# 56 short products behind the first products of ones, at the start of an attention and expert kernel

## The chip, the cores and the metric

The kernel runs on one core of a Trainium2 chip. Its time is device time in microseconds (us), as the median of several runs. The core has a matrix engine (TensorE, PE in the profile; its weight loads are listed apart as PEld), a vector engine (VectorE, DVE), a scalar engine (ScalarE, ACT), GpSimd (POOL) and SyncE (SP), whose queue issues most of the DMAs.

## What is computed

The reference joins two blocks. The first is linear attention without a softmax over 8 batches, 8 heads, 576 rows and 64 columns a head, followed by a normalisation of each row of a head:

```python
kv = np.einsum('bhsd,bhse->bhde', k, v)
out = np.einsum('bhsd,bhde->bhse', q, kv)
rms = np.sqrt(np.mean(out * out, axis=-1, keepdims=True) + 1e-06)
return (out / rms * g_norm).astype(np.float32)
```

Its result, laid out as 4608 tokens of 512, is the input of the second. Each token gets one of 8 experts: all pairs of token and expert are taken in falling order of their logits, and a pair is accepted if the token is free and the expert holds fewer than 576 tokens. Then each expert works on its own tokens:

```python
logits = x @ w_gate
...
h = np.maximum(x[mask] @ w1[e], 0.0)
out[mask] = h @ w2[e]
```

## The kernel before

**Attention.** A batch's Q, K and V are loaded in two halves each, of 576 KB, by `load` (line 84). The order is K, V, Q of the first half and then of the second. The first two batches are issued at once, the batch `b + 2` at the end of the function `prepare(b)`. `paced` (line 76) lets a load wait for the one three before it. For each batch `prepare` does, on TensorE: the sums K'V of four pairs of heads (`sum_kv`, line 342, whose products are on line 346), the turning of Q (`turn_q`, line 327, products on line 331), the turning of the sums (line 385) and the product of the sums with the gate's weights (line 395). `tiles` (line 410) multiplies the turned Q by the sums (line 434), and ScalarE, VectorE and GpSimd normalise the result. The main loop (lines 512 to 529) takes a piece of `prepare(b + 1)` behind every piece of the work on batch `b`, so that the two alternate on TensorE.

The order of instructions on TensorE, VectorE, ScalarE and SyncE is that of the program text in this part (`tc.manual_schedule`, line 508). TensorE starts with batch 0 alone, since nothing else is loaded: `prepare(0)` runs to its end first. Between its steps stand products of a tile of ones by another (`ones`, line 266), 9, 3, 4 and 3 of them. Each multiplies `ones_b` (128 by 128, bf16) by `wide` (128 by 512, bf16) into the first half of `begun`, a tile of PSUM. Nothing reads that half. The second half of `begun` takes the bound on the gate's logits (`gate_bound`, line 280).

Each product on TensorE is two instructions in the program, a weight load (LDWEIGHTS) and the product itself (MATMUL).

**Experts.** After the attention part the kernel chooses the experts' tokens by a search for thresholds (lines 575 to 700 or so; its counting products, of 128 by 32 weights with 8 columns, are on line 584), gathers the tokens, and multiplies them expert by expert (lines 1005, 1110 and 1124), with the second product's results scattered to the output by GpSimd (line 922). A last block, `exactly`, is there for inputs on which the search didn't settle; a branch passes it here.

The change touches `prepare` and adds a function beside `ones`.

Of the kernel before, what the change touches and what calls it, by code (L numbers as in the profile page):

```python
# [28 lines left out]
def kernel(  # L29
# [11 lines left out]
    nc = tc.nc  # L41
# [4 lines left out]
    E, _, F = moe_w1.shape  # L46
# [37 lines left out]
    def load(name, b, h):  # L84

        if h == 0:
            loaded[name, b] = att.tile([P, NP, R, D], FT, name=f"{name}_sb", tag=name, bufs=2)
        rs = slice(h * NP // 2, (h + 1) * NP // 2)
        src = {"k": k, "v": v, "q": q}[name]
        paced(nc.sync.dma_start(  # L90
            loaded[name, b][:, rs].rearrange("p r j d -> p r (j d)"),
            src[b].rearrange("h s d -> (h s) d").rearrange("(r p j) d -> p r (j d)", r=NP, j=R)[:, rs]))
# [50 lines left out]
    ones_b = asg.tile([P, P], BF, name="ones_b")  # L143
    nc.vector.memset(ones_b, 1.0)
    wide = asg.tile([P, 512], BF, name="wide")
# [118 lines left out]
    begun = psa.tile([P, 2, 512], FT, name="begun_ps", tag="o", bufs=2)  # L264

    def ones(times):

        for _ in range(times):
            nc.tensor.matmul(begun[:, 0], lhsT=ones_b, rhs=wide, start=True, stop=True)

    g2_ps = begun[:, 1, 0:E]

    def gate_norms():

        nc.vector.tensor_scalar(gw.rearrange("p r l e -> p (r l e)"), in0=gw.rearrange("p r l e -> p (r l e)"),
                                scalar1=g_col, scalar2=None, op0=AL.mult)
        nc.vector.tensor_tensor(gsq, gw.rearrange("p r l e -> p (r l e)"), gw.rearrange("p r l e -> p (r l e)"), op=AL.mult)
        nc.vector.reduce_sum(out=g2, in_=gsq.rearrange("p (a e) -> p e a", e=E), axis=AXX)
# [39 lines left out]
    def prepare(b):  # L318

        k_sb, v_sb = loaded.pop(("k", b)), loaded.pop(("v", b))  # L320

        q_sb = loaded.pop(("q", b)).rearrange("p r j d -> p (r j d)")
        NT = NP * R // 2
        qt = att.tile([P, 2, NT, HP], FT, name="qt", tag="qt", bufs=3)
        turned_q[b] = qt

        def turn_q(n):
            m = min(4, NT - 4 * n)
            t_ps = psa.tile([P, 4, P], FT, name="qt_ps", tag="tr", bufs=2)
            for x in range(m):  # L330
                nc.tensor.transpose(t_ps[:, x, :], q_sb[:, (4 * n + x) * P:(4 * n + x + 1) * P], ident)  # L331

            to, got = qt[:, :, 4 * n:4 * n + m], t_ps[:, 0:m].rearrange("p x (l c) -> p l x c", l=2)
            if n in (1, 2):
                nc.vector.tensor_copy(to, got)
            else:
                nc.scalar.copy(to, got)


        kv_ps = psa.tile([P, 2, 512], FT, name="kv_ps", tag="kv")  # L340

        def sum_kv(r):
            for j in range(R):
                for l in range(2):
                    ls, cs = slice(l * D, (l + 1) * D), slice(j % 2 * D, (j % 2 + 1) * D)
                    nc.tensor.matmul(kv_ps[cs, l, r * D:(r + 1) * D], lhsT=k_sb[ls, r, j, :], rhs=v_sb[ls, r, j, :],  # L346
                                     start=(j < 2), stop=(j >= R - 2))

        if b == 0:
            ones(9)  # L350
            sum_kv(0)
            sum_kv(1)
            ones(3)
            turn_q(0)
            turn_q(1)
            gate_norms()
            ones(4)
        else:
            sum_kv(0)
            turn_q(0)  # L360
            yield
            sum_kv(1)
            turn_q(1)
            if b % 2 == 0:
                yield
        sum_kv(2)
        sum_kv(3)
        odd = att.tile([D, 2, NP * D], FT, name="odd", tag="odd")
        nc.scalar.copy(odd, kv_ps[D:P, :, 0:NP * D])
        kv = att.tile([D, NP, 2, D], FT, name="kv", tag="kv")  # L370
        nc.vector.tensor_tensor(kv.rearrange("p r l d -> p l r d"),  # L371
                                kv_ps[0:D, :, 0:NP * D].rearrange("p l (r d) -> p l r d", d=D),
                                odd.rearrange("p l (r d) -> p l r d", d=D), op=AL.add)

        kvx = att.tile([P, H, W], FT, name="kvx", tag="kvx", bufs=3)
        for n in range(2):
            nc.gpsimd.tensor_copy(kvx[n * D:(n + 1) * D, :, 0:D], kv.rearrange("p r l d -> p (r l) d"))  # L377
        if b > 0:
            yield
        else:  # L380
            ones(3)
        turn_q(2)
        t_ps = kv_ps[:, 0, NP * D:2 * NP * D].rearrange("p (r d) -> p r d", d=D)
        for r in range(NP):
            nc.tensor.transpose(t_ps[:, r, :], kv[:, r].rearrange("p l d -> p (l d)"), ident[0:D, 0:D])
        kvt = att.tile([P, NP, D], FT, name="kvt", tag="kvt")
        nc.scalar.copy(kvt, t_ps)
        if b > 0:
            yield
        else:  # L390
            turn_q(3)
        w_ps = kv_ps[:, 1, NP * D:NP * D + NP * 2 * E].rearrange("p (r x) -> p r x", r=NP)
        for r in range(NP):
            for n in range(2):
                nc.tensor.matmul(w_ps[n * D:(n + 1) * D, r], lhsT=kvt[:, r, :],
                                 rhs=gw[:, r].rearrange("p l e -> p (l e)"), start=True, stop=True)
        nc.vector.tensor_copy(kvx[:, :, D:W], w_ps.rearrange("p r (l e) -> p (r l) e", l=2))
        kv_of[b] = kvx
        if b > 0:
            turn_q(3)  # L400
        turn_q(4)
        if b + 2 < B:
            for h in range(2):
                for name in "kvq":
                    load(name, b + 2, h)
# [102 lines left out]
    with tc.manual_schedule(engines={PE, DVE, ACTE, SPE}):  # L508
        for _ in prepare(0):
            pass  # L510
        gate_bound()
        for b in range(B):
            parts = prepare(b + 1) if b + 1 < B else iter(())
            n = 0
            tile_work = work(b)
            for _ in tile_work:
                next(parts, None)
                n += 1
                if b == 0 and n == 1:
                    columns()  # L520
                for _ in range(((0, 1, 2, 2), (0, 1, 2, 0, 2))[b % 2][n - 1] if b + 1 < B else (0, 1, 1, 0, 0)[n - 1]):
                    chosen()
            while b + 1 == B and choices:
                chosen()
            for do in late:
                do()

            while b + 2 >= B and writes:
                writes.pop(0)()
# [845 lines left out]
```

## Time and profile before

| | us |
|---|---|
| median of 3 runs | 606.0 |
| lowest and highest run | 605.68 and 615.02 |
| the profiled execution's own time | 605.56 |
| its span, from the first to the last instruction | 603.7 |
| mean granted clock of TensorE | 0.971 |
| TensorE busy (products) | 569.0, 4524 instructions |
| TensorE busy (weight loads) | 448.9, 4524 instructions |
| VectorE, ScalarE, GpSimd busy | 388.0, 184.4, 413.2 |

The span is 1.86 us shorter than the profiled execution's time. The attention part takes the first 110 us or so, the choice of the tokens the next 25, the experts the rest.

The profile's views are read like this. The page gives each engine's busy time and count of instructions, and the span in 40 slices of 15.1 us, whose digits are tenths (9 is 90% or more); the row PEclk is the clock that TensorE was granted. In a timeline a row has the start in us, the length in us, the engine, the line of the program, the operation, the output and inputs, the shape, the count of instructions merged into the row, and in square brackets the idle time ahead of it with what ended that. The chain of waits is the work that ended last, followed back from the end; "issue" in it is time in which an engine waited for nothing that the profile shows. A row of windows has the window, its length, then for PE, PEld, DVE, ACT and POOL the busy time and in brackets the count of instructions, and last the granted clock, the share of the DMA engines and GB/s.

### The profile page before, as it was taken

The page shows a single profiled execution, that of the slowest core. Times are in us where ns is not written, and L with a number is a line of the kernel's source. Part 1 is how long each engine was busy: PE and PEld are TensorE (multiplying, and loading weights), DVE is VectorE, ACT ScalarE, POOL GpSimd, SP SyncE. Part 2 cuts the span into 40 slices and gives each one's busy share as a digit, 9 for nine tenths or more (in the row PEclk, how much of TensorE's full clock was granted, in tenths as well). Part 3 has the DMA queues.
Part 4 walks back from the last instruction along what each step waited for, and adds up shares of the span by engine and source line. Part 5 has one row for each costly group of instructions (what it writes and reads, how often), then busy time and mean ns, then how long its engine had stood idle before and what let it go on. Part 6 is the DMA issues. An engine that isn't in the chain of part 4 may idle for free.

```text
span 603.7 us, 12101 instructions
## 1 busy us (share of the span) xinstructions
PE 569.0 (94%) x4524; PEld 448.9 (74%) x4524; DVE 388.0 (64%) x1195; ACT 184.4 (31%) x417; POOL 413.2 (68%) x367
## 2 busy tenths in 40 slices
PE   6899899458999999999999999999999999999995
PEld 3788788435788678867877786788678867877883
DVE  3676558768878797878767875887583355134411
ACT  1566456813221322232122203221322222223200
POOL 0146435215998989479969796987898699869523
PEclk9999799659999999999999999999999999999999
DMA  8998988948027169159538617580949364310002
GB/s 282 326 317 293 308 295 298 341 140 278 4 80 277 71 143 327 53 144 284 167 78 280 175 62 179 184 231 1 272 136 258 65 218 130 108 53 27 1 0 84
DMA packets 60932, 105.24 MB, mean 174 GB/s; under 512 B 5312, under 2 KB 19904, under 8 KB 60864
## 3 DMA queue, kind: packets, MB, share of 16 engines
q1 hardware_dynamic: 54272, 85.47, 45.2%
q0 software_dynamic: 5888, 18.88, 9.8%
q8 instruction: 38, 0.62, 0.4%
q14 instruction: 30, 0.25, 0.1%
q10 hardware_dynamic: 704, 0.02, 0.1%
HBM read 78.40 MB, written 25.95 MB: 173 GB/s over the span
## 4 chain that ended last, share of the span: by engine, by line
PE 83%; DVE 6%; DMA 4%; issue 3%; POOL 2%; ACT 1%; POOLq 0%; DVEq 0%; ACTq 0%
PE h_ps L1005 34%; PE y_ps L1110 32%; PE o_ps L434 5%; PE y_ps L1124 4%; PE kv_ps L346 3%; DMA v_sb<-in_v_dram 3%; PE qt_ps L331 2%; DVE ms L450 1%; PE given_ps L588 1%; DMA g_col<-in_g_norm_dram 1%; PE given_ps L584 1%; DMA xg<-x_dram,ids 1%; PE t_ps L913 1%; POOL out_dram L922 1%; POOL sw L935 0%
## 5 line engine op out<-in xcount | busy, mean ns | idle before, releaser
L1005 PE MATMUL h_ps<-xt,w_sb 128*128 128x288 f32 x384 | 101.1, 412 | 0.9 <-ACT xt L916 0.8
L1017 ACT ACTIVATE hid<-hid 128x288 f32<-128x288 f32 x128 | 55.6, 443 | 149.9 <-DVE hid L1000 148.0
L1005 PEld LDWEIGHTS h_ps<-xt,w_sb 128*128 128x128 f32 x384 | 70.8, 190 | 24.9 <-issue 4.9
L1000 DVE TENSOR_TENSOR hid<-h_ps,u 128x288 f32<-128x288 f32 x128 | 56.8, 453 | 28.5 <-PE h_ps L1005 24.5
L1005 PE MATMUL h_ps<-sx,sw 128*128 128x288 f32 x256 | 68.1, 407 | 0.1
L811 POOL DMA_INDIRECT xg<-x_dram,ids x40 | 38.2, 955 | 33.9 <-DVE upper L641 21.7
L1110 PE MATMUL y_ps<-tw,hid 128*128 128x256 f32 x256 | 59.2, 381 | 0.0
L1110 PE MATMUL y_ps<-tw,sh 128*128 128x256 f32 x256 | 59.1, 381 | 0.0
L1005 PEld LDWEIGHTS h_ps<-sx,sw 128*128 128x128 f32 x256 | 48.3, 190 | 13.8 <-DVE u L1000 0.6
L1110 PE MATMUL y_ps<-w_sb,hid 128*128 128x256 f32 x256 | 58.3, 382 | 0.0
L475 POOL TENSOR_TENSOR xo<-o_sb,inv 128x512 f32<-128x512 f32 x31 | 32.5, 1077 | 30.3 <-ACT o_sb L442 12.7
L1110 PEld LDWEIGHTS y_ps<-w_sb,hid 128*128 128x128 f32 x256 | 48.0, 190 | 6.7
L1110 PEld LDWEIGHTS y_ps<-tw,sh 128*128 128x128 f32 x256 | 48.2, 190 | 6.4
L1110 PEld LDWEIGHTS y_ps<-tw,hid 128*128 128x128 f32 x256 | 48.1, 190 | 6.5
L1000 DVE TENSOR_TENSOR u<-h_ps,u 128x288 f32<-128x288 f32 x96 | 42.1, 450 | 11.4 <-PE h_ps L1005 9.0
L922 POOL DMA_INDIRECT out_dram<-y_sb,outs x32 | 31.7, 989 | 22.7 <-issue 21.6
L907 ACT ACTIVATE xt<-t_ps,g_two 128x256 f32<-128x256 f32 (+1 forms) x60 | 23.9, 450 | 65.0 <-DVE t_ps L904 56.7
L434 PE MATMUL o_ps<-kvx,qt 64*128 64x72 f32 (+1 forms) x640 | 41.1, 274 | 2.8 <-issue 1.4
L434 PEld LDWEIGHTS o_ps<-kvx,qt 64*128 64x128 f32 (+1 forms) x640 | 36.2, 182 | 7.0 <-issue 5.5
L935 POOL TENSOR_TENSOR tw<-w_sb 128x512 f32<-128x512 f32 x32 | 40.0, 1271 | 0.1
L1000 DVE TENSOR_TENSOR y_sb<-y_ps,u 128x512 f32<-128x512 f32 x24 | 16.5, 687 | 31.0 <-PE y_ps L1110 30.7
L377 POOL COPY kvx<-kv 64x512 f32<-64x512 f32 x16 | 9.8, 610 | 37.5 <-DVE kv L371 37.0
(216 smaller groups left out, 1065.8 us busy)
## 6 DMA issues: line engine op xcount, KB each, us to landing
w_sb<-in_moe_w_dram SPq DMA_DIRECT2D x8, 2048.0 KB
w_sb<-in_moe_w_dram SPq DMA_DIRECT2D x48, 256.0 KB
k_sb<-in_k_dram SPq DMA_DIRECT2D x16, 576.0 KB
v_sb<-in_v_dram SPq DMA_DIRECT2D x16, 576.0 KB
q_sb<-in_q_dram SPq DMA_DIRECT2D x16, 576.0 KB
x_dram<-xo SPq DMA_DIRECT2D x16, 512.0 KB
relaid<-xg SPq DMA_DIRECT2D x24, 256.0 KB
xr<-relaid SPq DMA_DIRECT2D x24, 256.0 KB
```

Source lines behind the costliest of these rows:

```text
L346: nc.tensor.matmul(kv_ps[cs, l, r * D:(r + 1) * D], lhsT=k_sb[ls, r, j, :], rhs=v_sb[ls, r, j, :], start=(j < 2), stop=(j >= R - 2))
L434: nc.tensor.matmul(o_ps[rows_at, rp, (2 * r2 + l) * W:(2 * r2 + l + 1) * W], lhsT=turned_q[bn][ks, l, block // 2:block // 2 + m].rearrange ...
L475: nc.gpsimd.tensor_tensor(xo[t // 2][:, t % 2], o_sb[:, t, :, 0:D], inv[:, t * H:(t + 1) * H].rearrange("p (h o) -> p h o", o=1).to_broadc ...
L811: tokens = nc.gpsimd.indirect_dma_start(out=xg[0:nr], out_offset=None, in_=x_dram, in_offset=bass.IndirectOffsetOnAxis(ap=ids[0:nr, n:n + ...
L907: nc.scalar.mul(xt[:, q::2, a:a + nr], t_ps[:, q::2, 0:nr], g_two[:, q:q + 1])
L922: put = nc.gpsimd.indirect_dma_start(out=out, out_offset=bass.IndirectOffsetOnAxis(ap=ids_of[t][0:nr, n:n + 1], axis=0), in_=y_sb[0:nr, :] ...
L935: in_order(nc.gpsimd.tensor_tensor(o, x, y, op=op))
L1000: nc.vector.tensor_tensor(o, p_ps, u, op=AL.add)
L1005: nc.tensor.matmul(o, lhsT=left[:, d, f * P:(f + 1) * P], rhs=right[:, d], start=d == 0, stop=d == KH - 1)
L1017: nc.scalar.activation(h, h, ACT.Relu)
L1110: nc.tensor.matmul(p_ps[:, n], lhsT=left[:, f, n * P:(n + 1) * P], rhs=right[:, f], start=(f == 0), stop=(f == FH - 1))
L1124: nc.tensor.matmul(y_ps[l * nr:(l + 1) * nr], lhsT=hid[:, l * FH + f, a:a + nr], rhs=w2[:, l * FH + f, :], start=(f == 0), stop=(f == FH - 1))
```

## The change

A function `short` is added beside `ones`. It issues products of the first 32 columns of `ones_b` by the first 8 columns of `wide`, into 32 rows and 8 columns of the half of `begun` that nothing reads. In `prepare(0)` it is called with 56, behind the first nine products of ones and ahead of the first sums. These are 56 weight loads and 56 products more in TensorE's stream. Nothing is removed or moved.

```diff
         for _ in range(times):
             nc.tensor.matmul(begun[:, 0], lhsT=ones_b, rhs=wide, start=True, stop=True)
 
+    def short(times):
+
+        for _ in range(times):
+            nc.tensor.matmul(begun[0:32, 0, 0:8], lhsT=ones_b[:, 0:32], rhs=wide[:, 0:8], start=True, stop=True)
+
     g2_ps = begun[:, 1, 0:E]
...
         if b == 0:
             ones(9)
+            short(56)
             sum_kv(0)
             sum_kv(1)
             ones(3)
```

## The prediction

> **What bounds the kernel now.** I read the page first, then the timeline of the first 25 us, the chain of waits, and windows of the stretches that these pointed to. From the page:
>
> ```profile
> span 603.7 us, 12101 instructions
> PE 569.0 (94%) x4524; PEld 448.9 (74%) x4524; DVE 388.0 (64%) x1195; ACT 184.4 (31%) x417; POOL 413.2 (68%) x367
> PEclk9999799659999999999999999999999999999999
> PE 83%; DVE 6%; DMA 4%; issue 3%; POOL 2%; ACT 1%; POOLq 0%; DVEq 0%; ACTq 0%
> q8 instruction: 38, 0.62, 0.4%
> ```
>
> TensorE carries 83% of the chain that ended last, so whatever is to change the time must shorten or lengthen TensorE's own stream, in a stretch where nothing else ends later. The clock is whole except in the slices around 60 to 90 us and 105 to 135 us. The change sits far ahead of both. The beginning, in the timeline of TensorE:
>
> ```profile
> 1.69 3.91 PE L269 MATMUL begun_ps<-wide,ones_b 128*128 128x512 bf16 x9 [1.69 <-DVE wide L146]
> 7.26 1.38 PE L346 MATMUL kv_ps<-v_sb,k_sb 64*64 64x64 f32 x72 [1.67 <-DMA v_sb<-in_v_dram]
> 12.64 1.38 PE L346 MATMUL kv_ps<-v_sb,k_sb 64*64 64x64 f32 x72 [1.15 <-DMA v_sb<-in_v_dram]
> 18.89 0.80 PE L346 MATMUL kv_ps<-v_sb,k_sb 64*64 64x64 f32 x36 [0.24 <-DMA v_sb<-in_v_dram]
> 24.14 1.38 PE L346 MATMUL kv_ps<-v_sb,k_sb 64*64 64x64 f32 x72 [0.85 <-DMA v_sb<-in_v_dram]
> ```
>
> The nine products of ones end at 5.60; the first real products start at 7.26, when V has landed. Three more waits for V follow, 1.15, 0.24 and 0.85 us, the last ending at 24.14. The chain of waits says the same and goes on:
>
> ```profile
> 12.61 6.14 DMA v_sb<-in_v_dram
> 18.77 5.24 DMA v_sb<-in_v_dram
> 24.14 1.38 PE kv_ps L346 x70
> ...
> 46.91 0.49 issue
> ...
> 63.30 1.61 issue
> ...
> 86.40 1.41 issue
> ...
> 99.23 1.31 PE kv_ps L346 x70
> ```
>
> Up to 24 us the chain is loads, and TensorE's delays vanish in it. From 24 us TensorE itself is the chain. In it stand three holes, 3.51 us in all, in which TensorE waits for nothing that the profile shows ("issue"), in the middle of groups of equal products. What they are is the main question here, since the change adds 112 instructions to TensorE's stream (56 weight loads, 56 products) and nothing else.
>
> **What the holes are.** Windows cut at the holes, whose counts in brackets are the products (first) and the weight loads (second) in each:
>
> ```profile
> 10.80:47.30 36.50, 32.67 (x762) 27.50 (x760) 24.63 (x72) 20.13 (x41) 11.29 (x14) 1.00 0.96 325
> 47.30:64.50 17.20, 15.64 (x381) 13.76 (x380) 12.15 (x31) 11.36 (x22) 8.45 (x10) 1.00 0.91 307
> 64.50:87.50 23.00, 21.49 (x379) 18.80 (x380) 13.30 (x37) 11.05 (x22) 10.41 (x11) 0.78 0.92 303
> ```
>
> Between the holes lie 761 and 759 instructions, and 1522, twice as many, back to 10.8. Holes that come at equal counts belong to the stream and not to the work. The page's queue q8 carries instructions in 38 packets, 0.62 MB together and so 16 KB each. A third of 761 is 254, and TensorE's 9048 (4524 weight loads and as many products) instructions are 35.6 times 254, near those 38. I take it that the stream arrives in pages of about 254 counted instructions, that entering one page asks for the next, and that a hole is a page that isn't there when the one before is used up. [...]
>
> How long a page takes is bounded by the stretches that end at the holes, which begin one page ahead of them, and by the quickest page without a hole:
>
> ```profile
> 41.73:47.30 5.57, 5.17 (x126) 4.42 (x127) 3.96 (x9) 3.40 (x7) 3.46 (x4) 1.00 0.93 312
> 58.99:64.50 5.51, 4.30 (x134) 3.75 (x134) 4.04 (x9) 4.24 (x8) 1.98 (x3) 1.00 0.94 333
> 80.05:87.50 7.45, 6.34 (x133) 5.45 (x130) 5.95 (x17) 4.92 (x10) 3.92 (x4) 1.00 0.90 301
> 87.80:92.27 4.47, 4.46 (x125) 4.01 (x128) 1.46 (x4) 2.88 (x6) 0.73 (x2) 1.00 0.80 243
> ```
>
> The holes end at 46.91 + 0.49 = 47.40, 64.91 and 87.81, so those pages took 5.7, 5.9 and 7.8 us from the entry of the one before; the last row had its page in at most 4.5. While the loads keep the DMA engines 90 to 96% busy, a page thus takes some 4.5 to 5.9 us, once 7.8, and TensorE uses one up in 4 to 6: it is close to starved all through the attention part.
>
> **The short products themselves.** Two rows are nearest: products of the very same shape (128 by 32 weights, 8 columns, bf16), from the chain, at half clock, and products with 64-column weights at full clock:
>
> ```profile
> 119.44 1.45 PE given_ps L584 x36
> 16.40 0.65 PE L395 MATMUL kv_ps<-gw,kvt 128*64 128x16 f32 x16
> ```
>
> That is 40 ns each at half clock; halved for the full clock 20 ns is the lower end, and the second row's 41 ns, an overestimate since it holds the last product's way out, agrees with the upper. 56 of them take 1.1 to 2.3 us and end between 6.7 and 7.9; I take 1.7, which ends about when V lands. At the worst the first sums start 0.6 us late. They have until 12.64: the wait of 1.15 there swallows it, and if that cover were gone, 0.24 and 0.85 us come behind it. No engine waits on the products' result and no DMA is issued by them; SP's and POOL's queues are not passed. Nothing below zero comes from here either: the sums can't start ahead of V. This term is 0.
>
> **The moved pages.** Each page edge behind the insertion now comes 112 instructions earlier in the work. The hole at 46.91 shows where: 113 counted instructions ahead of it is 45.13. From there on a page at a time (instructions that overlap an edge are counted on both sides of it):
>
> ```profile
> 45.13:47.30 2.17, 1.78 (x57) 1.40 (x56) 1.13 (x2) 1.13 (x2) 2.17 (x3) 1.00 0.91 289
> 45.13:49.31 4.18, 3.69 (x128) 3.25 (x128) 1.16 (x3) 1.71 (x3) 3.98 (x4) 1.00 0.91 305
> 56.62:60.53 3.91, 3.91 (x134) 3.53 (x134) 2.18 (x5) 2.46 (x5) 3.13 (x4) 1.00 0.89 275
> 69.40:76.16 6.76, 6.76 (x128) 5.85 (x129) 1.54 (x3) 1.71 (x3) 4.37 (x5) 0.50 0.93 295
> 83.82:89.55 5.73, 4.32 (x130) 3.90 (x131) 2.96 (x7) 2.31 (x5) 3.95 (x4) 1.00 0.86 293
> ```
>
> The three old holes go: -3.5 us. Against a page time of 4.5 to 5.9 us, the new page from 45.13 holds 4.18 - 0.49 = 3.7 us of work: a hole of 0.8 to 2.2. The one from 56.62 holds 3.9: 0.6 to 2.0. The one from 83.82 holds 5.73 - 1.41 = 4.3: 0.2 to 1.6. The rest of the new pages have 5 us or more, or lie past the loads. Together 1.6 to 5.8, middle 3.7. Net -1.9 to +2.3, middle +0.2.
>
> **The clock behind a hole.** The second hole is followed by a slow stretch:
>
> ```profile
> 66.00:67.00 1.00, 1.00 (x16) 0.84 (x14) 0.72 (x3) 0.95 (x3) 0.00 (x0) 0.91 0.91 336
> 76.00:78.00 2.00, 2.00 (x35) 1.81 (x29) 0.69 (x2) 0.67 (x2) 0.00 (x0) 0.74 0.97 345
> 60.28 1.05 PE o_ps L434 x16
> 70.03 1.92 PE o_ps L434 x16
> ```
>
> The clock, 0.50 between these windows, falls at 66.8 (0.91 of a window whose end runs at 0.5) and is back at 77.0: 10.2 us. The last two rows are the same group in the chain of waits, 1.92 us in the stretch against 1.05 ahead of it. So 0.55 of the slow time would have done, and the stretch costs 10.2 x 0.45 = 4.6 us. The holes of 0.49 and 1.41 us are followed by no fall. [...] My reading is that a hole of about 1.6 us can bring it on, depending on where it lies against some window. A new hole of up to 2.0 us after 60.53 is the heir of the old one at 63.30, at nearly the same place and of the same size. I expect the fall to stay, a few us earlier, at the same price: 0.
>
> **The sum.** 0 + 0.2 + 0 on the profiled execution's 605.56 us (603.7 of span and 1.86 around it), which is 0.4 under the median of 606.0 of runs from 605.68 to 615.02: about 606.0 on the median's scale.
>
> **Rivals.** (1) The fall of the clock goes: the new hole behind 60.53 is shorter, or is cut by a window's edge as the one at 86.40 may be. TensorE gains 4.6 us, if loads allow:
>
> ```profile
> 88.81 0.37 SPq L90 DMA_DIRECT2D v_sb<-in_v_dram  x1
> ```
>
> The last V is issued at 88.81; at the 5.2 us that such a load took at 18.77 it lands at 94.1, and it is used at 99.23, so up to 5.1 us can be won there before loads bind. But the page from 69.40 then holds 6.76 x 0.55 = 3.7 us and gets a hole of 0.8 to 2.2, say 1.5. -4.6 + 0.2 + 1.5 = -2.9: 603.1, between 600.5 and 605. For it: two of three holes brought no fall. (2) Slower: a second fall. It takes a hole of about 1.6 us at 49.31 or 89.55 as well, both within the upper end of their ranges; +0.2 + 4.6 = 610.8, more if the page of 7.8 us recurs. (3) The holes go not by count but by the DMA's load at that moment, and moving the edges does nothing: 606.0. Against it stand the equal counts. (4) The short products end so late that first sums pass 12.64: they would need over 1.15 + 1.67 = 2.8 us, 50 ns each, and even then 24.14 still takes the delay; I give it no chance of its own.
>
> **Chances.** Forecast 0.42 (604 to 608), clock's fall gone 0.27, second fall 0.18, nothing moves 0.08, and 0.05 for what lies past 2%. Two per cent, 12 us, is about what a measurement of this kernel can tell from no change. To go past it downward all holes and more than the clock's fall would have to go (0.02); upward takes three falls (0.04 with the second rival's tail). The range reaches over rivals 1 and 2 without their ends: 601 to 611.5.
>
> **What would show it.** Right: short products from about 5.6, the first sums at 7.3 to 7.9, a wait for V still ending at about 12.6 and 24.1; no hole at the groups that held the old ones, and new ones 112 instructions earlier in the work modulo a page, near 49 and 61; a stretch of half clock of some 10 us near 63 to 74. Wrong: a start of the fifth V group later than 24.2; holes still at the same groups; the end of the attention part (last use of V, 99.23) off by over 3 us; any difference behind 140 us.

## The result, and the profile after

The first measurement gave 613.22 us as the median of 4 runs (609.41 to 614.48) against 605.84 us of the kernel before (4 runs, 605.31 to 615.02); the ratio is 1.0116, interval 1.0073 to 1.0158. That lies above the range. In three later measurements of 10 to 12 runs each beside 29 to 31 of the kernel before, the ratio came out at 0.9992 (0.9944 to 1.0041), 1.0005 (0.9957 to 1.0053) and 0.9955 (0.9901 to 1.0009). These ratios leave out the runs over 1.5% above the fastest of a kernel, so that a kernel without a fast run keeps all of its runs (e10 and e14 below); here those runs are the upper end of one wide scatter, and medians over all runs stand beside the ratios: 607.8 us over 34 runs with the change, 612.0 over 88 without it, measured together. One more run of the kernel before took 1173.78 us at full clock; it is in none of the figures over several measurements. The change made no slower kernel; whether the lower median is a gain the ratios leave open. What the first eight runs showed is what this document has to explain.

The page of the changed kernel, in the profiled execution (612.97 us):

```profile
span 611.2 us, 12210 instructions
PEclk9997579958999999999999999999999999999999
PE 81%; DMA 8%; DVE 5%; POOL 2%; issue 2%; ACT 1%; POOLq 0%; ACTq 0%; DVEq 0%
```

Loads have gone from 4% to 8% of the chain, "issue" from 3% to 2%, and the clock's dip is wider. The beginning, in TensorE's timeline:

```profile
5.31 1.55 PE L274 MATMUL begun_ps<-wide,ones_b 128*32 128x8 bf16 x56
7.22 1.38 PE L351 MATMUL kv_ps<-v_sb,k_sb 64*64 64x64 f32 x72 [0.36 <-DMA v_sb<-in_v_dram]
13.58 1.38 PE L351 MATMUL kv_ps<-v_sb,k_sb 64*64 64x64 f32 x72 [2.10 <-DMA v_sb<-in_v_dram]
23.59 1.38 PE L351 MATMUL kv_ps<-v_sb,k_sb 64*64 64x64 f32 x72 [0.32 <-DMA v_sb<-in_v_dram]
```

The 56 products took 1.55 us, 28 ns each, and end at 6.86, ahead of V. The first sums start at 7.22 (7.26 before), and TensorE still waits for loads at 13.58 and 23.59. So the beginning costs nothing. The chain of waits further on:

```profile
41.76 5.44 DMA v_sb<-in_v_dram
47.19 0.14 issue
47.33 1.38 PE kv_ps L351 x70
48.71 1.04 PE o_ps L440 x15
49.75 0.83 issue
...
67.91 1.91 PE o_ps L440 x16
...
84.84 1.05 PE o_ps L440 x16
...
106.15 1.31 PE kv_ps L351 x70
```

Without the old holes TensorE keeps up with the loads, which stay the chain up to 47 us (24 before). Then one hole of 0.83 us comes at 49.75, and no other of that kind follows in the attention part. But the group on line 440 takes 1.91 us at 67.91 and 1.05 only at 84.84. The last use of V comes at 106.15, where it was at 99.23: 6.9 of the span's 7.5 us are lost by then. Windows show where; first two of the changed kernel, then two of the kernel before:

```profile
49.32:52.73 3.41, 2.58 (x34) 2.12 (x32) 2.85 (x8) 1.41 (x4) 1.83 (x3) 1.00 0.91 295
52.73:83.45 30.72, 30.72 (x413) 26.71 (x412) 13.61 (x36) 13.31 (x26) 10.65 (x11) 0.50 0.90 300
```

```profile
63.40:66.81 3.41, 1.91 (x27) 1.71 (x28) 2.23 (x7) 1.86 (x5) 0.00 (x0) 1.00 0.94 326
66.81:77.05 10.24, 10.24 (x184) 8.96 (x181) 3.53 (x8) 3.59 (x8) 5.26 (x5) 0.50 0.90 289
```

The clock, last number but two, fell at 52.73 and stayed at half for 30.72 us, against 10.24 before; TensorE was busy all the time in both. Of the 20.5 us more, 0.45 is lost (the share worked out in the prediction): +9.2. A hole of 0.83 us in the place of 3.51 us of holes gives -2.7. The sum, +6.5, is near the 6.9 lost by the last use of V. The lengths are 3 and 9 times 3.41 us. The later stretches at half clock, during the choice of tokens, are 7 and 6 times as long; first the kernel before, then the changed one:

```profile
111.18:135.08 23.90, 10.47 (x165) 6.81 (x165) 17.00 (x60) 11.73 (x45) 1.91 (x3) 0.50 0.60 224
```

```profile
120.99:141.47 20.48, 9.19 (x147) 6.06 (x145) 14.88 (x54) 9.22 (x39) 1.01 (x1) 0.50 0.42 159
```

The full clock between them, from 77.05 to 111.18 and from 83.45 to 120.99, lasts 10 and 11 times 3.41 us. So all changes of the clock in these two profiles lie a whole number of 3.41 us apart, and the windows of 3.41 us below are counted off from such a change. In the kernel before one begins at 87.29 (77.05 + 3 x 3.41), inside the hole of 1.41 us from 86.40 to 87.81.

### The profile page after: what moved, and what is told of

Its sections match the earlier page's. It is cut to its first block, busy times and chain, and to the rows that moved or that the text cites. A ratio compares the mean times of both kernels' runs of the same rounds, so it can differ in the third digit from the quotient of the medians.

```text
span 611.2 us, 12210 instructions
## 1 busy us (share of the span) xinstructions
PE 577.8 (95%) x4577; PEld 457.5 (75%) x4580; DVE 387.8 (63%) x1195; ACT 184.5 (30%) x417; POOL 412.5 (67%) x367
## 4 chain that ended last, share of the span: by engine, by line
PE 81%; DMA 8%; DVE 5%; POOL 2%; issue 2%; ACT 1%; POOLq 0%; ACTq 0%; DVEq 0%
PE h_ps L1011 34%; PE y_ps L1116 31%; DMA v_sb<-in_v_dram 7%; PE y_ps L1130 4%; PE o_ps L440 4%; PE kv_ps L351 3%; PE qt_ps L336 2%; DVE ms L456 1%; PE given_ps L594 1%; PE given_ps L590 1%; DMA g_col<-in_g_norm_dram 1%; DMA xg<-x_dram,ids 1%; PE t_ps L919 1%; POOL out_dram L928 1%; POOL sx L941 0%
## 5 line engine op out<-in xcount | busy, mean ns | idle before, releaser
L440 PE MATMUL o_ps<-kvx,qt 64*128 64x72 f32 (+1 forms) x640 | 44.9, 295 | 2.1 <-DVE kvx L403 1.3
L440 PEld LDWEIGHTS o_ps<-kvx,qt 64*128 64x128 f32 (+1 forms) x640 | 39.8, 201 | 7.0 <-issue 5.8
```

The costliest lines, as they stand in the source:

```text
L440: nc.tensor.matmul(o_ps[rows_at, rp, (2 * r2 + l) * W:(2 * r2 + l + 1) * W], lhsT=turned_q[bn][ks, l, block // 2:block // 2 + m].rearrange ...
```

## The experiments

My theory after this: the difference is the time that the clock is down, which one hole sets off and chance then stretches; page edges decide where holes fall. The rivals: the short products cost by themselves; filling the first wait is what costs; the edges don't matter and all is chance.

Every run has a span and a mean clock; 2 x (1 - clock) x span is its time at half clock, since the kept traces have no value of the clock but 0.5 and 1. (They have none at all ahead of 4 to 15 us into the span; that stretch counts as full. In the kernel before the first value begins at 5.37. Nine wide products of ones took 3.91 us nearly all ahead of it, 0.43 each, and four took 1.03 us behind it, 0.26 each.) For the kernel before, over 130 runs in five measurements, that time and the run's time go together with a correlation of 0.94: 594 us, and 0.37 us for each us at half clock. The four runs of the changed kernel in the first measurement have 46 to 61 us, 52.5 in the mean; of the kernel before only the profiled execution has its clock on record there, 35 us. At 0.37 us each the difference makes some 6.4 of the 7.4 us between the medians. All kernels that ran, with the median of the kernel before that was measured beside them:

| kernel | us, median (runs) | before | ratio, interval | us at half clock, mean |
|---|---|---|---|---|
| before, all five measurements | 612.3 (130) | | | 48 |
| e1, 128 short | 607.3 (10) | 610.3 | 0.999, 0.9945 to 1.0035 | 44 |
| e2, 56 short in the second wait | 613.3 (10) | 610.3 | 1.0049, 0.9984 to 1.0115 | 51 |
| e3, 16 wide | 613.9 (10) | 610.3 | 0.9965, 0.9901 to 1.0029 | 53 |
| e4, the change | 608.5 (10) | 610.3 | 0.9992, 0.9944 to 1.0041 | 41 |
| e5, 2 loads in flight | 630.2 (4) | 612.4 | 1.0322, 1.0237 to 1.0408 | 78 |
| e6, 4 loads | 606.5 (10) | 612.4 | 0.9997, 0.9938 to 1.0057 | 34 |
| e7, short in each batch | 615.4 (11) | 612.4 | 1.0056, 0.9998 to 1.0115 | 50 |
| e8, wide in each batch | 609.6 (10) | 612.4 | 0.9962, 0.9913 to 1.0011 | 35 |
| e9, the change | 607.2 (12) | 612.5 | 1.0005, 0.9957 to 1.0053 | 42 |
| e10, 6 loads | 612.8 (6) | 612.5 | 1.0133, 1.008 to 1.0186 | 47 |
| e11, 4 loads, wide in each batch | 612.0 (12) | 612.5 | 1.0066, 1.0019 to 1.0113 | 39 |
| e12, 4 loads and the change | 617.2 (12) | 612.5 | 1.002, 0.9949 to 1.0091 | 56 |
| e13, 4 loads | 608.4 (12) | 612.9 | 1.0009, 0.9957 to 1.0062 | 38 |
| e14, 4 loads and the change | 617.4 (6) | 612.9 | 1.0134, 1.0065 to 1.0204 | 59 |
| e15, the change | 607.8 (12) | 612.9 | 0.9955, 0.9901 to 1.0009 | 47 |
| e16, 88 short | 603.5 (12) | 612.9 | 0.9921, 0.9877 to 0.9965 | 31 |
| e17, 88 short | 600.9 (7) | 610.7 | 0.988, 0.9826 to 0.9934 | 29 |
| e18, 24 short | 613.4 (12) | 610.7 | 0.9949, 0.9868 to 1.003 | 52 |

Of the time at half clock 20 to 24 us in each profile are the choice of tokens behind the attention part, which no kernel here touches.

**Whole page, other place, other filling, and the change again (e1 to e4).** Against the changed kernel:

```diff
 e1
-            short(56)
+            short(128)
 e2
             ones(9)
-            short(56)
...
             ones(4)
+            short(56)
 e3
-            ones(9)
-            short(56)
+            ones(16)
```

> 128 short products in the place of the 56: 256 instructions, one whole page of the instruction stream, so that every later page edge falls on the same work as in the kernel before. If the moved page edges are what costs the 7.4 us: holes (issue on TensorE) at the old groups, near 47, 63 and 86 us, one slow stretch of about 10 us of half clock, and 606 +- 1.5 us. If the short products cost by themselves, by their work or by what they do to the clock at the start: more of them cost more, 613 us or above, with a long slow stretch again.

> The 56 short products moved into the second wait for V (behind the four products of ones, ahead of the third sum): the same page edges as with the change from there on, but nothing at all in the first wait. If the page edges cost: a hole near 49 us as with the change, and 609 to 615 us. If it is the filled first wait that costs: back to 606 us.

> Seven more wide products of ones (16 in all) in the place of the 56 short ones: the first wait is filled for the same 1.5 us, with 14 instructions in the place of 112. If the page edges cost, these hardly move: holes near 47, 63 and 86 us and 604 to 608 us. If the filled wait costs: 613 us.

> The changed kernel once more, for how much chance there is in one execution. If the slow stretch of 30.7 us follows from where the hole falls in the work: again a hole of about 0.8 us near 49.8, a slow stretch of about 30 us from about 53, and 611 to 614 us. If it is chance, from where the hole falls against a clock window that isn't bound to the kernel's start: another length, between 10 and 40 us, and a time that follows it by 0.45 us for each.

The medians say little at first: all four, and the kernel before, scatter over 602 to 625 us. The profiles say more. In e1, with 256 instructions put in, TensorE's timeline has this, and the timeline of the kernel before that:

```profile
63.89 0.41 PE L401 MATMUL kv_ps<-gw,kvt 128*64 128x16 f32 x6
65.90 0.82 PE L401 MATMUL kv_ps<-gw,kvt 128*64 128x16 f32 x10 [1.60 <-issue]
```

```profile
62.89 0.41 PE L395 MATMUL kv_ps<-gw,kvt 128*64 128x16 f32 x6
64.90 0.52 PE L395 MATMUL kv_ps<-gw,kvt 128*64 128x16 f32 x10 [1.61 <-issue]
```

The hole is behind the sixth of the same sixteen products (line 401 is line 395 moved by six lines). With 112 instructions it was elsewhere, with 256 it is back to the instruction: for this hole 256 more instructions do what a whole page (254 counted instructions) would. Of the other two old holes none came back in e1 (0.35 us and less elsewhere). In e2 three holes stand in the chain, and windows from the end of one to the end of the next count them off:

```profile
34.50 1.21 issue
51.84 1.30 issue
81.52 1.02 issue
```

```profile
35.71:53.14 17.43, 16.13 (x380) 14.29 (x380) 11.17 (x27) 8.71 (x17) 8.37 (x11) 0.90 0.95 312
53.14:82.54 29.40, 28.38 (x508) 24.89 (x508) 15.37 (x41) 14.59 (x29) 10.65 (x12) 0.71 0.86 280
```

760 and 1016 instructions, about three and four times 254. The traces show more than these two cases. In all 20 profiles together TensorE has 64 holes of 0.2 us and more in the attention part that no engine or load ends. Numbered along TensorE's stream, every one stands at the 181st to 189th instruction of a run of 254, and every one ends 1.2 to 1.75 us behind the end of a 16 KB packet on the queue of instructions. In the kernel before these packets ended at 46.09, 63.63 and 86.43 us and the three holes at 47.39, 64.90 and 87.81. So a hole is a page that came late. The first rival falls too: more than twice the short products (e1) cost nothing that can be measured. e3, with 16 wide products, has holes near 47, 64 and 85 us as expected and four more; its median, 613.9 us, lies where the second rival put it, but its ten runs scatter from 604.0 to 623.8 and the ratio shows no cost.

e4 is the changed kernel to the letter, and its profiled execution took 602.32 us. From its page, its chain, and its windows:

```profile
span 600.5 us, 12213 instructions
```

```profile
72.21 1.42 issue
```

```profile
70.55:73.96 3.41, 1.99 (x78) 1.62 (x76) 0.69 (x1) 0.27 (x1) 3.38 (x4) 1.00 0.96 308
73.96:77.38 3.42, 3.42 (x56) 3.08 (x56) 2.62 (x7) 2.40 (x5) 1.23 (x2) 1.00 0.85 274
```

Same program, and no hole at 49.75; a longer one at 72.21, 1.42 us, and one of 0.67 us at 85.46, with no fall of the clock behind either. What I expected if it was chance came true, outside the span of 10 to 40 us that I had written: no half clock at all in the attention part. Two executions of the same program differ by 10.7 us of span, one with 30.7 us of half clock in that part and one with none. The two further profiles of the change fit in: none in e9 (602.59 us), 17.1 us in e15 (607.52 us).

**Loads in flight (e5, e6, e10).** If pages of instructions queue behind packets of loads, fewer loads in flight should end the holes.

```diff
-    AHEAD = 3
+    AHEAD = 2        # e5; 4 in e6, 6 in e10
```

> The kernel before with two loads in flight in the place of three (AHEAD 2). If the holes are pages of instructions that queue behind load packets, a shorter queue brings them earlier: holes on TensorE together under 1.5 us in the attention part, where the kernel before has 3.5, a fall of the clock there in few runs or none, and times drawn together near the lowest seen, 600 to 606 us, with little spread. If holes and falls have nothing to do with the loads' queue: the same scatter of 603 to 625 us. If two in flight starve the loads, waits for V and Q grow and the time goes up with the clock whole.

> The kernel before with four loads in flight. If pages queue behind load packets: more and longer holes than 3.5 us in all, longer stretches of half clock, a median above that of the kernel before by 2 to 8 us. If the queue doesn't matter: no difference.

> The kernel before with six loads in flight. With four the median came down to 606.5 from 612.4 us and the time at half clock from 50 to 34 us a run. If more loads in flight keep TensorE from waiting for V and so from losing the clock: 603 to 607 us, no worse than with four. If the pages of instructions queue longer behind six loads: holes of 2 us and more, and 612 us or above.

All that TensorE waited for in e5 between 5 and 125 us, and the attention part as one window, first of e5, then of e6:

```profile
PE kv_ps L346 <- DMA v_sb<-in_v_dram: 8.2, 6, 2.5
PE qt_ps L331 <- DMA q_sb<-in_q_dram: 6.4, 6, 1.9
PE o_ps L434 <- DVE kvx L397: 1.0, 3, 0.4
```

```profile
5.00:110.00 105.00, 92.67 (x1789) 79.30 (x1791) 54.73 (x152) 48.54 (x97) 31.51 (x36) 0.82 0.81 244
```

```profile
5.00:110.00 105.00, 96.65 (x2110) 83.12 (x2109) 66.33 (x182) 58.69 (x116) 40.63 (x46) 0.93 0.93 333
```

With two loads in flight not one hole is left, as the theory said. But the loads come at 244 GB/s in the place of 311 in the kernel before, TensorE waits 14.6 us for V and Q, the clock falls behind these waits as well (0.82 in the mean), and the time is 630 us. So a wait for loads can go ahead of a fall as a hole can. For four loads the theory expected more holes and a slower kernel. The holes in e6's profile are 4.2 us in all, a little more than 3.5, but the half clock went from 50 to 34 us a run and the median down by 6 us; the ratio shows no difference (0.9997). With six loads the holes that the theory expected are there, 6.8 us in all and one of 2.3, but the median is that of the kernel before (612.8 and 612.5 us, though the ratio is 1.0133). In these single profiles the holes do grow with the loads in flight (0, 3.5, 4.2 and 6.8 us for 2, 3, 4 and 6); the times don't follow them.

**More instructions, or denser work (e7, e8).** At the head of each later preparation, against the kernel before, into columns of the sums' tile that are overwritten later:

```diff
         else:
+            for _ in range(32):                      # e7
+                nc.tensor.matmul(kv_ps[0:32, 0, 256:264], lhsT=ones_b[:, 0:32], rhs=wide[:, 0:8], start=True, stop=True)
+            for _ in range(8):                       # e8, in its place
+                nc.tensor.matmul(kv_ps[:, 0, 256:512], lhsT=ones_b, rhs=wide[:, 0:256], start=True, stop=True)
             sum_kv(0)
```

> The kernel before with 32 short products at the head of each of the seven later preparations, 448 instructions and 6 us of TensorE in all, results unread. If TensorE is starved for instructions, each costs a quarter of a page beside its own time: more holes and more half clock, the median up by 8 us or more, and by more than in the kernel with wide products of the same length. If only TensorE's time counts: up by at most 6 us, the same as there.

> The kernel before with 8 wide products (256 columns, all of the array) at the head of each of the seven later preparations: also 0.9 us each and 6 us in all, but 112 instructions in the place of 448. If the starving for instructions decides: up by less than with the short products. If dense products keep the clock up or bring it back, the slow stretches get shorter and this may come out even with the kernel before, or under it.

Medians of 615.4 and 609.6 us for nearly the same time of TensorE (0.95 to 1.05 us a batch at full clock): the kernel with 448 instructions put in is slower by 5.8 than the one with 112. The window of e8's attention part:

```profile
5.00:110.00 105.00, 99.46 (x2115) 84.28 (x2114) 63.27 (x178) 56.83 (x114) 38.07 (x43) 0.97 0.93 315
```

TensorE is busy for 99.5 of 105 us, against 94.9 before by the same window, and the half clock is down from 50 to 35 us a run. The time won there and the 7 us of work that the wide products cost about cancel. That it is their density that helps the clock isn't shown: the 112 instructions move the page edges as well, and no run here has the one without the other.

**More runs, and the two together (e9, e11, e12).** e9 is the changed kernel again, e11 is e8 with four loads in flight, e12 the changed kernel with four.

> The changed kernel, with more runs beside the kernel before on the same chip. If the first difference (1.0116) came from how long the clock happened to be down in four runs of each: medians within 3 us of each other, both scattered over some 602 to 620 us. If the change does cost something in most runs: a median 4 to 8 us above that of the kernel before.

> Four loads in flight, and the 8 wide products at the head of each later preparation. The wide products alone cost 6 us of TensorE and gave 609.6 us with half clock down to 35 us a run. If both keep the clock up by separate ways: hardly any half clock left in the attention part, about 25 us a run for the choice of tokens, and 602 to 607 us with little scatter. If they do the same thing: 606 to 610 us.

> The change (56 short products) with four loads in flight. If the page edges that it moves matter for the median: off by over 3 us from the 606.5 of four loads alone. If they only deal the holes anew: 604 to 609 us, the same scatter.

e9 had a median 5 us under the kernel before and a ratio of 1.0005. In e11 the two together brought nothing, 612.0 us with 39 us of half clock. e12 was the surprise: the change, which does no harm with three loads in flight, stood 10.7 us above four loads alone, but on another chip.

**The odds (e13 to e18).** So the same two on one chip, the change once more, and 88 and 24 short products in the place of 56.

```diff
-            short(56)
+            short(88)        # e16, e17; 24 in e18
```

> Four loads in flight without short products, now on the same chip as with them. If the edges of the pages set the odds of a fall of the clock: again near 606 us, and 6 us or more under the kernel with both. If the 606.5 against 617.2 us of the two earlier calls was the chip or chance: the two within 3 us of each other.

> Four loads in flight and the 56 short products, beside the one without them. If the edges set the odds: 613 us or more again, with 10 us or more of half clock a run above the other. If it was the chip or chance: within 3 us of it.

> The changed kernel a third time beside the kernel before. So far 22 runs of it have a median of 607.8 us and 60 runs of the kernel before 611.1 in the same calls, though the comparisons gave 0.9992 and 1.0005. If the moved edges lower the odds of a fall: again 2 to 6 us under the median of the kernel before, with less half clock. If it is chance: a difference under 2 us or of the other sign.

> 88 short products, 176 instructions: the edges of the pages lie 64 instructions further on than with 56, 80 short of where they were before. The work in the first wait grows by 0.9 us, which the second wait takes. If the edges set the odds: a median off by over 3 us from that with 56. If not: the same median as with 56 and as before, within 2 us.

> 88 short products once more, since 603.5 us was the lowest median of all kernels. If the odds of a fall go with the edges: again 602 to 606 us, and 6 us or more under the median of the kernel before. If the first was chance: 606 to 612 us.

> 24 short products, 48 instructions: edges 48 instructions earlier in the work than before, 64 short of where the change puts them. If the odds go with the edges, a median of its own, off from both 612 and 608 us, to either side; by the nearer neighbour, the kernel before, 609 to 615 us.

e13 and e14 came out as e6 and e12 had: 608.4 and 617.4 us, 38 and 59 us of half clock. Five of the six runs of e14 lie above all twelve of e13, on one chip. That is hardly chance: with four loads in flight, 56 short products in a wait of the first 8 us change how long the clock is down later. The profiles have it between 50 and 104 us: 10 to 14 us of half clock without the short products (e6, e13), 34 to 38 with them (e12, e14). The change alone: 607.8 against 612.9 us, and 0.9955. 88 short products gave 603.5 and then 600.9 us; both intervals lie wholly under 1, by about 1%, and in e16 the kernel is faster than the changed one measured beside it (607.8). What its TensorE waited for between 5 and 110 us in e16, and that window:

```profile
PE o_ps L440 <- DVE kvx L403: 1.6, 5, 0.4
PE qt_ps L336 <- DMA q_sb<-in_q_dram: 1.4, 2, 0.7
PE kv_ps L351 <- DMA v_sb<-in_v_dram: 1.3, 4, 0.5
PE kv_ps L351 <- issue: 0.6, 1, 0.6
PE kv_ps L391 <- DVE kv L377: 0.2, 1, 0.2
```

```profile
5.00:110.00 105.00, 98.08 (x2198) 84.69 (x2197) 66.73 (x183) 59.52 (x118) 41.41 (x47) 0.93 0.92 310
```

In this execution there is one hole of 0.6 us where the kernel before had three of 3.5 together, and no wait for a load over 0.7 us. That isn't the rule for the kernel: the profile of e17 caught the longest of its seven runs, 611.22 us, with holes of 3.3 us in all, one of them 2.5, and 20.5 us of half clock behind that one. e18, with 24, is no different from the kernel before.

The profiles of 88 short products also show a fall of the clock with no wait ahead of it. Two windows of e16:

```profile
5.45:8.86 3.41, 3.41 (x155) 3.28 (x156) 0.00 (x0) 0.00 (x0) 0.00 (x0) 1.00 0.83 303
8.86:12.27 3.41, 3.41 (x33) 2.55 (x22) 0.00 (x0) 0.55 (x1) 0.00 (x0) 0.50 1.07 376
```

TensorE was busy for the whole first window, mostly with the short products, and the clock was at half in the second. e17 has the same at 8.72.

The second rival, that nothing but chance is at work, falls with e13 against e14 and with e16 and e17. That it is the page edges by which the short products act is possible and not shown: e2 has the edges of the change from the second wait on, and its median is 613.3 us beside e4's 608.5, measured together. What the short products do to the beginning itself, as in the windows of e16, is a rival that no run here separates from the edges.

## Why the prediction was wrong

**The short products and the beginning: right.** 1.55 us (1.7 taken, 1.1 to 2.3 bounded), an end ahead of V, and waits for loads ahead of 13.58 and 23.59 that hide everything. Halving the 40 ns for the full clock was no sound bound, though: e7 has such products in stretches of both clocks, and they take nearly the same time.

```profile
61.64 1.01 PE L360 MATMUL kv_ps<-wide,ones_b 128*32 128x8 bf16 x32
79.07 0.95 PE L360 MATMUL kv_ps<-wide,ones_b 128*32 128x8 bf16 x32
```

The first row lies at half clock (54.04 to 74.52), the second at full.

**Pages: right, and rival 3 is refuted.** The hole of e1 at the same sixth product, the counts of e2 and the 64 holes of all profiles show that holes go by the count. The packets show it too: in the kernel before, TensorE passes 14 edges, 254 counted instructions apart, from 10.47 to 92.32 us, and behind each of them one packet of 16,384 bytes starts, 1.2 to 5.4 us later.

**The new holes: one of three.** The one near 49.31 came at 49.75, 0.83 us long (0.8 to 2.2 forecast). Those near 60.5 and 89.5 didn't. The first of these two edges lies in the slow stretch now, where TensorE took 7.2 us over the page. But that is not all of the reason: in e4 TensorE did the same page at full clock in 3.94 us, as the prediction had it, and there is no hole either.

```profile
58.05:61.99 3.94, 3.94 (x134) 3.56 (x136) 1.71 (x4) 2.52 (x5) 1.70 (x2) 1.00 0.86 266
```

The other edge, at 96.50 in the changed kernel, lies 13 us behind the slow stretch, and its packet had ended 1.3 us before. The 4.5 to 5.9 us for a page came from pages that were late, and others come faster. So the term for the new holes, 1.6 to 5.8 us, was too large: it measured 0.83 us here, and 2.1, 1.0 and 2.4 in e4, e9 and e15. The hole near 60.5 is in none of the four.

**The clock: here the prediction failed.** The step is "I expect the fall to stay, a few us earlier, at the same price: 0". The hole behind 60.53 that was to be the heir didn't come. A fall came all the same, at 52.73, 14 us ahead of the old one, behind a hole of 0.83 us that the prediction had taken for too short. Its price was 30.7 us of half clock and not 10.2: the term put at 0 came to +9.2 us. Nor is there one price: the four profiled executions of the change have 30.7, 0, 0 and 17.1 us.

What sets off a fall is known in part. A hole of 0.83 us was followed by one and a hole of 1.42 us in e4 by none, each inside one 3.41 us window, so the length of the hole alone doesn't decide. It counts for much, though: of the holes in all profiles, all 11 of 1.5 us and more were followed by a fall, at the end of a 3.41 us window in which they lie in whole or in part, 13 of 25 between 0.8 and 1.5 us, and 1 of 28 shorter ones. Of the 33 falls in the first 104 us, 25 have a hole in the 3.41 us ahead of them, five a wait for a load of 1.2 us or more, one several short waits, and two no wait at all (e16 and e17). What sets the length of the slow stretch stays open.

**The rivals.** The measured 613.2 us is near the second (610.8), by another way: one long fall and no second. The first, no fall, is what e4's execution shows, at 602.3 us (603.1 forecast), with the hole that this rival put at the end of the page from 69.40: 1.42 us at 72.21 (1.5 taken).

**The base: also wrong.** I took 605.56 and 606.0 us for the kernel's time, since three of four figures agreed within 0.5 us. Over 130 runs its median is 612.3 us, from 601.5 to 629.7, and 17% of them are at or under 606.0. The fourth figure, 615.02, lies well inside that. The first comparison set three good draws of the kernel before against four of the changed kernel that all lie above its median of 607.8. "About zero" was nearer to the truth of the change than the 1.0116 was, but not by its reasons, since the holes and the falls came otherwise than it summed them; that is luck. The range was drawn round one execution's luck, and with the scatter known it would have had to reach from 602 to 620.

## What to carry to other kernels

Where TensorE runs many small products beside heavy loads, count its instructions: the holes at equal counts here (254 or a multiple), each 1.2 to 1.75 us behind a packet of instructions, were pages that came late, and 112 instructions put in moved the edges behind them. When a profile shows a slow stretch of the clock, look at many runs with their clocks before taking its length, or the time, for a property of the kernel. An edit that adds cheap instructions in a wait can be worth trying at several counts (24, 56, 88 and 128 here), as long as each is measured over enough runs.

## What the runs showed of the hardware

- A late page of instructions stops TensorE: 64 holes of 0.2 to 2.65 us, at every 254 counted instructions or a multiple, each ending 1.2 to 1.75 us behind the end of a 16 KB packet. With two loads in flight (244 GB/s) there were none.
- The clock can stay at half for 30.7 us while TensorE shows no idle time, and it can fall behind 3.41 us without idle time, when these are mostly products of 32 weight columns with 8 columns (e16, e17). What sets off such a fall isn't settled.
- A late first rise of the clock cost nothing that the times of e1 show (607.3 against 610.3 us, ratio 0.999). Its first record of the clock begins at 14.29; before that the first sums took 2.40 us for the group that took 1.38 in the kernel before, 1.74 times as long, where the group on line 440 above took 1.82 times as long in the slow stretch (1.91 and 1.05 us), though the profile counts such a stretch without record as full. Its profiled execution took 604.89 us:

```profile
5.62 3.58 PE L274 MATMUL begun_ps<-wide,ones_b 128*32 128x8 bf16 x128
9.12 2.40 PE L351 MATMUL kv_ps<-v_sb,k_sb 64*64 64x64 f32 x72
```

- Short products came at 28 ns each there and at 28 ns (1.55 us for 56) in the changed kernel, and at 32 and 30 ns in the two stretches of e7 above, at half and at full clock. For this shape the clock hardly set the pace.
- A hole of 0.83 us was followed by a slow stretch that cost some 14 us (30.7 x 0.45), seventeen times its length; the same program also ran without either.
